# Splitting the first eight steps into float32r parts, with a new hand-written order for the first layers

## Chip, core and metric

One core of one Trainium2 chip runs the whole program. The metric is the device time of one execution in microseconds (us). The engines are named as the profile names them: PE is TensorE, DVE is VectorE, ACT is ScalarE, POOL is GpSimd, and SP issues the DMAs.

## What is computed

Three layers follow each other. The first is attention through 32 memory slots, for 4 batches `b` of 576 positions and 8 heads:

```python
a = softmax(phi, axis=2)                       # over the 576 positions
k_m = einsum('bhsm,bhsd->bhmd', a, k)          # 32 keys of 64
v_m = einsum('bhsm,bhsd->bhmd', a, v)
attn = softmax(q @ k_m.T / 8)                  # over the 32 slots
x = attn @ v_m                                 # 2304 tokens of 512, heads side by side
```

The second is a dense pair of products, and the third four weighted experts:

```python
h = x @ w_in                                   # 512 -> 2048
x = (maximum(h, 0) + alpha * minimum(h, 0)) @ w_out
for e in range(4):
    out += p[:, e:e+1] * (maximum(x @ w1[e], 0) @ w2[e])
```

`w_in` and `w_out` arrive as 64-bit floating-point numbers, which the kernel decodes on the chip into float32 before it uses them.

## The kernel before

The kernel has two parts. `run_experts` is the third layer; the diff doesn't touch it. The first two layers run before it as a list of tasks in the string `ORDER`: each name is a task, and the tasks are emitted in that order with the scheduler switched off. Each engine has its own queue and works it off in order, so the string sets, for every engine, what stands behind what.

The second layer is cut into 128 steps. A step is a block of 128 of the 2048 inner columns for half a batch (288 tokens). Step `j` counts blocks fastest (4 of them, `f`), then halves, then batches, then the four groups `c` of 512 inner columns, so steps 0 to 7 are `c=0, b=0`. The attention product with `v_m` is folded into `w_in`: `f{b}{c}{e}` (line 523) multiplies `v_m` of a batch with 256 decoded columns of `w_in` on PE, `fh` rounds the result to a float32r part (ACT, line 534), and `fl` makes the remainder (DVE, line 232). A step has these tasks:

- `u{j}`, PE: the product with the attention weights, line 559 if plain and line 562 if split
- `n{j}`, ACT: negative and positive part (lines 575 and 576), and `v{j}`, DVE: their sum with `alpha` (line 581)
- `h{j}`, ACT, rounds the result to a float32r part (line 585), and `l{j}`, DVE or POOL, makes the remainder (line 232); plain steps have neither
- `d{j}`, PE: the product with `w_out`, line 597 if plain and line 600 if split; `e{j}` copies or adds four blocks after every fourth step (lines 611 and 613)

A split product is three float32r products of rounded parts and remainders. A plain one is one float32 product, which the trace records as two matmuls. `PLAIN = 1` makes the steps with `b=0, c=0` plain, and `down` then reads the decoded `w_out` from a tile of its own.

The attention of batch `b` is a chain of small tasks for its two groups of heads `g`: `a{b}{g}_max, exp, sum, nat, natc, mem, memc, memt, memtc, sc0, sc1, ev0, ev1`, followed by the softmax over the slots, `s{b}{g}{o}_max, sub, exp, sum, mul, back, hi, lo`. For batch 0 that softmax is done in two halves of 288 columns, for the others in one piece of 576. A tile of `w_in` or `w_out` is decoded by `in{i}_0..4` and `out{i}_0..4` (lines 459, 463, 469, 470, 477 and 496), and `out{i}_5` and `out{i}_6` split it into parts (lines 500 and 232). `ON_VECTOR` names those tasks which run on DVE; of the tasks that have a choice, the others run on POOL. `w0` to `w4` are warming products on an identity matrix (line 246). `x{b}h{i}` (ACT, line 668) and `x{b}l{i}` (DVE) prepare the experts' input, `wh01` and `wl01` their first weights (ACT line 701, DVE line 232), and `sp3` stores the last batch to device memory, ahead of the experts' first weighting loads (`p<-pd`) on the SP queue.

The raw tiles go through a ring of three buffers, so that a load of one starts when the decoding of the third one before it has read its raw bytes.

Of the kernel before, what the change touches and what calls it, by code (L numbers as in the profile page):

```python
# [23 lines left out]
PLAIN = 1  # L24
# [10 lines left out]
w0 p0 pal ppr kv0 pr0 pr1 pr2 q0 w1 p1 kv1 q1 a00_max a01_max a00_exp a01_exp a00_nat a00_sum a00_natc a01_nat a01_sum  # L35
  pgates a01_nath a01_natc w2 a01_nathc a01_mem in0_1 in0_0 a00_mem in0_2 a01_memc in1_1 in0_3 out0_1 in1_0 in1_2
  a01_memt a00_memc q01 p2 a01_memtc a00_memt out0_0 in1_3 a01_sc0 a00_memtc out0_2 q2 a00_sc0 a01_ev0 in0_4 w3 a00_ev0
  s010_max in1_4 s000_max s010_sub f000 a10_max s000_sub s010_exp a11_max w4 fh000 out0_3 s000_exp a10_exp s010_sum
  out0_4 a11_exp s000_sum a10_nat s010_mul a10_sum a10_natc a11_nat s000_mul s010_back a11_nath a11_natc a11_sum
  a11_nathc s000_back in2_1 u0 out0_5 in2_0 u1 n0 in2_2 a00_sc1 n1 in2_3 a01_sc1 v0 in2_4 in3_1 d0  # L40
v1 in3_0 in3_2 in3_3 in3_4 a01_ev1 out0_6 out1_1 a00_ev1 f001 s01288_max out1_0 out2_1 a10_mem out1_2 fh001 out3_1
  out1_3 s000_hi out1_4 u2 a10_memc kv2 out2_0 d1
n2 out2_2 out1_5 out2_3 s010_hi a11_mem s00288_max in4_1 out2_4 out3_0 out2_5 v2 s00288_sub d2
s01288_sub s00288_exp out3_2 s01288_exp a11_memc out1_6 s00288_sum u3 s01288_sum a10_memt out2_6 n3 a20_max a11_memt
  a10_memtc out3_3 a11_memtc a10_sc1 a20_exp s00288_mul p3 s01288_mul a10_sc0 out3_4 in5_1 v3 out3_5 s010_lo s01288_back
  d3
s00288_back s01288_hi out3_6 s00288_hi a10_ev0 s000_lo in6_1 u4 a10_ev1 e3 s01288_lo a11_sc1 s00288_lo s100_max s100_sub
  n4 a11_sc0 a11_ev1 s100_exp v4 u5 a11_ev0 d4
s110_max n5 s110_sub s100_sum s110_exp u6 f100 v5 n6 s110_sum d5
fh100 s100_mul s110_mul u7 s100_back f101 q3 v6 s100_hi s110_back n7 d6  # L50
pst s100_lo s110_hi fl100 fh101 s110_lo a20_nat a21_max u8 v7 a21_exp u9 fl101 d7
n8 a20_sum a21_sum a20_natc v8 n9 in4_0 a21_nat h8 v9 a21_nath e7 l8 u10 in4_2 a21_natc d8
in4_3 a21_nathc in5_0 h9 in5_2 a20_mem n10 l9 v10 in5_3 h10 a21_mem l10 a20_memc in6_0 a31_max in4_4 a31_exp in6_2 d9
kv3 a21_memc in5_4 a30_max in7_1 u11 a31_sum a30_exp in6_3 a20_memt n11 a30_sum in6_4 a21_memt a20_memtc d10
a21_memtc v11 out4_1 in7_0 a20_sc0 h11 in7_2 a20_sc1 a20_ev0 l11 u12 a20_ev1 s200_max a21_sc1 n12 s200_sub a21_sc0
  a21_ev1 s200_exp v12 d11
out5_1 a21_ev0 h12 s210_max l12 u13 s200_sum e11 s210_sub u14 d12
n13 s200_mul s210_exp v13 f200 s210_sum h13 n14 l13 u15 s200_back fh200 s210_mul d13
fl200 s200_hi n15 v14 f201 s200_lo s210_back h14 s210_hi a30_nat l14 a30_natc s210_lo d14
fh201 v15 fl201 h15 u16 l15 in7_3 d15  # L60
# [7 lines left out]
s310_sum n22 l21 fh300 s300_mul d21
fh301 s310_mul in10_1 s300_back u23 v22 s300_hi s310_back h22 s300_lo s310_hi l22 n23 s310_lo d22
fl300 v23 u24 fl301 h23 n24 u25 l23 in8_0 d23  # L70
n25 v24 in8_2 h24 u26 e23 l24 v25 u27 in8_3 d24
h25 in9_0 n26 l25 in9_2 n27 d25
v26 v27 h26 u28 h27 l26 l27 d26
n28 in9_3 v28 in10_0 h28 d27
l28 in10_2 u29 e27 in10_3 u30 in8_4 d28
n29 in9_4 n30 v29 f010 h29 v30 l29 h30 u31 fh010 l30 in10_4 d29
fl010 n31 in11_1 v31 out8_1 d30
in11_0 h31 in11_2 out9_1 u32 l31 in11_3 d31
# [1030 lines left out]
```

## Time and profile before

| | |
|---|---|
| Time, median of 3 runs | 1208.26 us (1206.77 to 1208.98) |
| Profiled execution, its own time | 1206.66 us |
| Its span (first to last instruction) | 1204.7 us |
| PE busy | 1170.1 us (97%) |
| DVE busy | 782.4 us (65%) |
| ACT busy | 468.0 us (39%) |
| POOL busy | 420.2 us (35%) |

The span is 2.0 us shorter than the execution's own time. The first two layers end 418.6 us after the span's start with the last product of step 127, and the experts fill the rest. The stages have different limits, so the shares above say little about any one of them; the rows below are cut by stage.

### The profile page before, as it was taken

What the parts mean: (1) busy time and instruction counts of PE and PEld (TensorE: products, weight loads), DVE (VectorE), ACT (ScalarE), POOL (GpSimd) and SP (SyncE); (2) the same over time, 40 slices, a digit from 0 to 9 for tenths busy, and PEclk for the clock granted to TensorE, in tenths of its full rate; (3) what the DMA queues carried; (4) which work ended last, traced back from release to release, by engine and by line L of the source; (5) the groups of instructions that cost most, each with busy time, mean ns of one, the idle gap of its engine ahead of it and who ended that gap; (6) DMA issues with size and microseconds to landing.
All of it is one profiled execution on the core that took longest, in us unless ns stands there. A gap on an engine that the chain in (4) does not pass through costs nothing.

```text
span 1204.7 us, 21401 instructions
## 1 busy us (share of the span) xinstructions
PE 1170.1 (97%) x8794; PEld 1123.2 (93%) x8794; DVE 782.4 (65%) x1433; ACT 468.0 (39%) x1017; POOL 420.2 (35%) x361
## 2 busy tenths in 40 slices
PE   7799999999999989999999999989999999999998
PEld 6478899998999989999999999989999999999998
DVE  6999997685457744555566566676456656656553
ACT  4557665545455533323232223233422223232320
POOL 2212111232000054444534435465443552553430
PEclk9899999999999999999999999989999999999999
DMA  9642122010000132111112111132112111111001
GB/s 376 250 160 83 54 87 71 19 53 18 1 1 1 56 97 92 55 54 53 46 48 69 37 54 36 64 124 75 53 47 62 54 46 45 58 41 63 36 29 70
DMA packets 22994, 82.46 MB, mean 68 GB/s; under 512 B 3312, under 2 KB 4336, under 8 KB 20976
## 3 DMA queue, kind: packets, MB, share of 16 engines
q1 hardware_dynamic: 22896, 81.09, 19.8%
q8 instruction: 69, 1.13, 0.4%
q14 instruction: 29, 0.24, 0.1%
HBM read 73.97 MB, written 7.11 MB: 67 GB/s over the span
## 4 chain that ended last, share of the span: by engine, by line
PE 87%; DVE 9%; DMA 2%; ACT 1%; issue 1%; SPq 0%; ACTq 0%; DVEq 0%
PE o L823 34%; PE y L600 14%; PE uy L732 12%; PE uw L732 8%; PE ux L732 8%; PE h L562 7%; PE pw L523 2%; DMA rawin<-in_w_in 2%; PE y L597 1%; DVE g L232 1%; DVE xt L660 1%; DVE pos L581 1%; DMA p<-pd 1%; DVE min L469 0%; DVE mout L469 0%
## 5 line engine op out<-in xcount | busy, mean ns | idle before, releaser
L823 PE MATMUL o<-g,w 128*128 128x288 f32 x3072 | 450.9, 296 | 1.1 <-DVE g L232 1.1
L823 PEld LDWEIGHTS o<-g,w 128*128 128x128 f32 x3072 | 423.2, 189 | 1.8 <-DVE g L232 1.6
L232 POOL TENSOR_TENSOR w<-raww,w 128x512 fp32r<-128x512 f32 (+1 forms) x96 | 150.3, 1580 | 260.4 <-ACT w L507 155.3
L835 DVE TENSOR_TENSOR acc<-o,acc 128x288 f32<-128x288 f32 x224 | 102.1, 456 | 189.0 <-PE o L823 189.0
L600 PE MATMUL y<-g,wout 128*128 128x288 f32 x1440 | 210.1, 298 | 2.6 <-DVE g L232 1.0
L600 PEld LDWEIGHTS y<-g,wout 128*128 128x128 f32 x1440 | 195.9, 188 | 12.6 <-ACT pos L576 4.2
L732 PE MATMUL uy<-x,w 128*128 128x288 f32 x1152 | 186.0, 297 | 8.0 <-DVE v L766 8.0
L732 PEld LDWEIGHTS uy<-x,w 128*128 128x128 f32 x1152 | 164.7, 189 | 9.4 <-DVE v L766 9.3
L770 ACT COPY v<-ux 128x288 f32<-128x288 f32 x64 | 25.6, 400 | 291.8 <-PE ux L732 288.5
L801 ACT CAST g<-h 128x576 fp32r<-128x576 f32 x128 | 83.3, 676 | 139.5 <-DVE h L795 139.5
L232 POOL TENSOR_TENSOR g<-h,g 128x576 fp32r<-128x576 f32 x64 | 92.8, 1451 | 127.8 <-ACT g L801 123.0
L732 PE MATMUL ux<-x,w 128*128 128x288 f32 x768 | 123.4, 296 | 2.5 <-ACT v L770 2.5
L732 PE MATMUL uw<-x,w 128*128 128x288 f32 x768 | 123.1, 296 | 0.1
L795 DVE SCALAR_TENSOR_TENSOR h<-h,p 128x576 f32<-128x576 f32 x128 | 109.4, 855 | 6.4 <-DMA p<-pd 3.3
L562 PE MATMUL h<-a,wp 128*128 128x288 f32 x720 | 111.6, 297 | 0.3
L732 PEld LDWEIGHTS ux<-x,w 128*128 128x128 f32 x768 | 109.3, 189 | 2.7 <-ACT v L770 2.7
L732 PEld LDWEIGHTS uw<-x,w 128*128 128x128 f32 x768 | 109.3, 189 | 0.3 <-DVE y L611 0.3
L562 PEld LDWEIGHTS h<-a,wp 128*128 128x128 f32 x720 | 100.0, 188 | 5.3 <-issue 3.0
L766 DVE TENSOR_TENSOR v<-uy,v 128x288 f32<-128x288 f32 x128 | 58.5, 457 | 69.9 <-PE uy L732 69.4
L581 DVE SCALAR_TENSOR_TENSOR pos<-neg,nal,pos 128x288 f32<-128x288 f32 x120 | 64.7, 542 | 58.3 <-ACT pos L576 57.8
L575 ACT ACTIVATE neg<-h 128x288 f32<-128x288 f32 x128 | 52.8, 413 | 83.1 <-PE h L562 76.3
L232 POOL TENSOR_TENSOR g<-pos,g 128x288 fp32r<-128x288 f32 x24 | 19.7, 823 | 182.7 <-ACT g L585 134.2
(116 smaller groups left out, 1184.3 us busy)
## 6 DMA issues: line engine op xcount, KB each, us to landing
raww<-in_w SPq DMA_DIRECT2D x64, 512.0 KB, 3.7
kv<-in_kv SPq DMA_DIRECT2D x8, 1152.0 KB, 8.4
rawin<-in_w_in SPq DMA_DIRECT2D x16, 512.0 KB, 3.7
rawout<-in_w_out SPq DMA_DIRECT2D x16, 512.0 KB, 3.7
p<-pd SPq DMA_DIRECT2D x16, 288.0 KB, 4.0
q<-in_q SPq DMA_DIRECT2D x3, 1152.0 KB, 15.9
out<-acc SPq DMA_DIRECT2D x12, 288.0 KB, 2.1
pe<-in_phi SPq DMA_DIRECT2D x4, 576.0 KB, 9.0
```

What stands on the lines that cost most here:

```text
L232: eng.tensor_tensor(out=out, in0=in0, in1=in1.bitcast(F32), op=ALU.subtract)
L562: mm(p, wp_t[b, c, f // 2][:, x, o2 + g * 256:o2 + g * 256 + 128], a_t[b][:, y, g, o:o + HB], start=(n == 0), stop=(n == 5))
L575: nc.scalar.activation(out=neg, in_=p, func=AF.Relu, scale=-1.0)
L581: nc.vector.scalar_tensor_tensor(out=pos, in0=neg, scalar=nal[:, ft:ft + 1], in1=pos, op0=ALU.mult, op1=ALU.add)
L600: mm(First.acc[d], w[:, x, d * 128:(d + 1) * 128], self.gt[:, y, 0:HB], start=(self.start and n == 0), stop=(self.stop and n == 2))
L732: mm(p, w[:, x, a, k], operand(self.b, i)[:, y, k], start=(start and n == 0), stop=(n == 5), skip_group_check=not start)
L766: nc.vector.tensor_tensor(out=out, in0=x, in1=y, op=ALU.add)
L770: nc.scalar.copy(out=self.v1_t, in_=self.x)
L795: nc.vector.scalar_tensor_tensor(out=h, in0=h, scalar=0.0, in1=p_t[self.g // 2, self.b], op0=ALU.max, op1=ALU.mult)
L801: nc.scalar.copy(out=g_t[self.g, self.b, self.hp][:, i, 0], in_=h)
L823: mm(self.p, w[:, x, i, d % 2 * 128:(d % 2 + 1) * 128], g, start=(m == 0), stop=(m == 11))
L835: nc.vector.tensor_tensor(out=a, in0=self.p, in1=a, op=ALU.add)
```

## The change

There are four edits. `PLAIN` goes from 1 to 0, so steps 0 to 7 become split steps: each gets `h` and `l`, its two plain products of `u` become six float32r products, and its four plain products of `d` become twelve. Their folds get `fl000` and `fl001`. The split parts of the attention weights of batch 0 and of the first four `w_out` tiles were made before too, for other steps, and are now needed by step 0 already.

`ORDER` is written anew. The attention of batches 1 and 2 comes earlier against the steps, the decoding of `w_in` tiles 7 to 11 and `w_out` tiles 4 to 7 comes later, and `kv2` (keys and values of batch 2) is loaded ahead of `w_out` tile 2.

`ON_VECTOR` changes. `s00288`, `s01288`, `s100` and `s110` do their `sub` and `mul` on POOL now. `s000_lo`, `s00288_lo`, `s010_lo` and `s200_lo` go from POOL to DVE. `out1_6` and `out2_6` go to DVE and `out2_4` to POOL; `in0_4` and `in1_4` change places. Of the new remainders `l0`, `l2`, `l3` and `l7` are on POOL, and `l1`, `l4`, `l5` and `l6` on DVE.

The warming products change from 11, 12, 5, 5, 8 to 11, 12, 6, 5, 4.

```diff
-PLAIN = 1
+PLAIN = 0
...
-v1 in3_0 in3_2 in3_3 in3_4 a01_ev1 out0_6 out1_1 a00_ev1 f001 s01288_max out1_0 out2_1 a10_mem out1_2 fh001 out3_1
...
+  a20_memt a21_memc a20_memtc a21_memt a20_sc0 a21_memtc a10_ev1 out2_5 out3_2 d0
...
-    for i, n in enumerate((11, 12, 5, 5, 8)):
+    for i, n in enumerate((11, 12, 6, 5, 4)):
```

On PE, at the first step. In the kernel before, two plain `u` products (`h`) and a score product (`pc`) stand ahead of step 0's plain `d` products (`y00000` to `y00003`, the first of the four is shown), then a fold and the memory products of batch 1 (`pm10`):

```order
L559 MATMUL h0000_400<-pe0_133,wp000_352 128x288 x2
L559 MATMUL h0001_406<-pe0_133,wp000_352 128x288 x2
L357 MATMUL pc001_415<-q0_147,kt00_301 64x288 x2
L357 MATMUL pc011_425<-q0_147,kt01_287 64x288 x2
L597 MATMUL y00000_433<-g0000_410,wholeout0_363 128x288
...
L523 MATMUL pw001_455<-win0_313,vt00_302 64x256 x2
L523 MATMUL pw001_455<-win0_313,vt01_288 64x256 x2
L325 MATMUL pm10_466<-kv10_164,pe1_162 32x128 x18
```

In the kernel after, on the same engine just ahead of step 0's first `d` products:

```order
L562 MATMUL h0003_606<-a0_422,wp001_555 128x288 x6
L305 MATMUL pnh2_619<-ident_102,pe2_280 64x128
L306 MATMUL pnh2_619<-ident_102,pe2_280 128x128
L325 MATMUL pm20_631<-kv20_417,pe2_280 32x128 x18
L325 MATMUL pm20_631<-kv21_418,pe2_280 32x128 x2
...
L342 MATMUL pt21_723<-ident_102,kvb21_713 128x128 x2
L357 MATMUL pc200_727<-q2_319,kt20_719 64x288 x2
L600 MATMUL y00000_739<-g0000_569,wout0_426 128x288 x3
```

The products of batch 2's memory (`pm20`, `pm21`) and its first scores (`pc200`) now stand ahead of step 0, and steps 0 to 3 have their `u` products done before it.

On DVE, at steps 16 and 17 (`pos0200`, `pos0201`). Before, between their sums, `w_out` tiles 4 and 5 are decoded (`mout`, `sout`):

```order
L581 SCALAR_TENSOR_TENSOR pos0200_1209<-neg0200_1208,nal_104,pos0200_1209 128x288
L469 SCALAR_TENSOR_TENSOR mout4_994<-mout4_994,sout4_995 128x512
L470 TENSOR_SCALAR sout4_995<-mout4_994 128x512
L232 TENSOR_TENSOR g0200_1221<-pos0200_1209,g0200_1221 128x288
L477 SCALAR_TENSOR_TENSOR sout4_995<-rawout4_879,sout4_995 128x512
L459 TENSOR_SCALAR sout5_1047<-rawout5_957 128x512
L496 TENSOR_TENSOR win1_913<-min7_942,sin7_943 128x4x128
L496 TENSOR_TENSOR mout4_994<-mout4_994,sout4_995 128x512
L581 SCALAR_TENSOR_TENSOR pos0201_1263<-neg0201_1262,nal_104,pos0201_1263 128x288
```

After, at the same two steps, softmax work of batch 3 (`rs310`, `pe3`):

```order
L581 SCALAR_TENSOR_TENSOR pos0200_1384<-neg0200_1383,nal_104,pos0200_1384 128x288
L394 TENSOR_REDUCE rs310_1400<-pe3_653 128x18
L395 TENSOR_SCALAR rs310_1400<-rs310_1400 128x18
L396 RECIPROCAL rs310_1400<-rs310_1400 128x18
L402 TENSOR_TENSOR pe3_653<-pe3_653,rs310_1400 128x576
L232 TENSOR_TENSOR g0200_1418<-pos0200_1384,g0200_1418 128x288
L581 SCALAR_TENSOR_TENSOR pos0201_1412<-neg0201_1411,nal_104,pos0201_1412 128x288
```

The decoding of those `w_out` tiles has moved to a place behind step 21.

On ACT, at the end of the second layer. Before, the last two castings of the experts' input (`x15`) stand between the last steps' parts (`g3312`, `g3313`) and the experts' first weights (`w101`):

```order
L585 CAST g3312_5037<-pos3312_4989 128x288
L668 CAST x15_5040<-xt1_4795 128x576
L585 CAST g3313_5043<-pos3313_5034 128x288
L668 CAST x15_5040<-y1_1066 128x576
L701 CAST w101_5090<-raww11_3148 128x768
```

After:

```order
L585 CAST g3312_5141<-pos3312_5108 128x288
L575 ACTIVATE neg3313_5144<-h3313_5111 128x288
L576 ACTIVATE pos3313_5145<-h3313_5111 128x288
L585 CAST g3313_5175<-pos3313_5145 128x288
L701 CAST w101_5208<-raww11_3617 128x768
```

Those two castings are done before step 118's product now, and nothing stands between the last step's part and the weights.

## Rows read from the trace of the kernel before

**Rows 1.** The page: span, and PE's busy time, share and instructions.

```profile
span 1204.7 us, 21401 instructions
PE 1170.1 (97%) x8794; PEld 1123.2 (93%) x8794; DVE 782.4 (65%) x1433; ACT 468.0 (39%) x1017; POOL 420.2 (35%) x361
```

**Rows 2.** Stages: from:to, length, busy us (instructions) by engine, clock, DMA, GB/s.

```profile
0.00:28.20 28.20, 22.11 (x202) 18.34 (x202) 18.47 (x46) 12.78 (x31) 6.63 (x17) 0.94 0.94 373
28.20:78.50 50.30, 43.08 (x272) 30.00 (x276) 46.09 (x90) 29.53 (x73) 8.06 (x7) 0.93 0.51 191
78.50:136.20 57.70, 52.28 (x490) 43.15 (x491) 56.34 (x106) 37.88 (x100) 14.80 (x13) 1.00 0.32 114
136.20:200.00 63.80, 63.72 (x475) 60.04 (x474) 56.05 (x113) 41.22 (x105) 9.47 (x8) 1.00 0.24 76
200.00:418.60 218.60, 217.69 (x1607) 203.21 (x1606) 146.17 (x295) 113.19 (x283) 33.23 (x33) 1.00 0.07 23
418.60:434.90 16.30, 12.67 (x79) 11.62 (x78) 7.60 (x15) 3.88 (x8) 5.08 (x5) 0.90 0.54 173
```

**Rows 3.** Chain that ended last, start and length, first 150 us.

```profile
36.27 0.76 DVE pe L362 x2
...
137.80 1.59 PE y L600 x12
139.39 1.58 PE h L562 x12
```

**Rows 4.** Timeline of PE: start, length, what, idle before it.

```profile
54.16 3.70 PE L597 MATMUL y<-g,wholeout 128*128 128x288 f32 x8 [2.00 <-DVE g L581]
...
65.17 2.21 PE L597 MATMUL y<-g,wholeout 128*128 128x288 f32 x8
67.22 1.13 PE L559 MATMUL h<-pe,wp 128*128 128x288 f32 x4
68.28 1.08 PE L523 MATMUL pw<-win,vt 128*64 128x256 f32 x8
...
78.43 2.80 PE L325 MATMUL pm<-kv,pe 128*32 128x128 f32 x80
```

**Rows 5.** Timeline of DVE: first row of one tile's decoding and of the next.

```profile
37.29 0.41 DVE L459 TENSOR_SCALAR sout<-rawout 128x512 uint32<-128x512 uint32 x1
...
40.33 0.42 DVE L459 TENSOR_SCALAR sout<-rawout 128x512 uint32<-128x512 uint32 x1
```

**Rows 6.** DVE and POOL groups, first 140 us: count, busy us, mean ns.

```profile
L232 DVE TENSOR_TENSOR g<-pos,g 128x288 fp32r<-128x288 f32 x13 | 7.3, 564 | 0.0
L385 DVE TENSOR_TENSOR pe<-pe,mx 128x576 f32<-128x576 f32 x5 | 3.7, 748 | 0.1
L385 POOL TENSOR_TENSOR pe<-pe,mx 128x576 f32<-128x576 f32 x1 | 1.2, 1169 | 0.0
L232 POOL TENSOR_TENSOR g<-pos,g 128x288 fp32r<-128x288 f32 x4 | 3.6, 900 | 11.0 <-ACT g L585 11.0
L232 POOL TENSOR_TENSOR wout<-wholeout,wout 128x512 fp32r<-128x512 f32 x3 | 4.3, 1427 | 15.1 <-ACT wout L500 15.1
```

**Rows 7.** Timeline of POOL and of DVE beside it, at two places.

```profile
20.66 1.59 POOL L385 TENSOR_TENSOR pe<-pe,mx 128x288 f32<-128x288 f32 x2 [4.27 <-DVE mx L379]
46.20 1.97 POOL L232 TENSOR_TENSOR a<-pe,a 128x288 fp32r<-128x288 f32 x2
...
21.36 1.40 DVE L276 TENSOR_REDUCE nm<-pe 128x1 f32<-128x576 f32 x2
46.47 2.02 DVE L385 TENSOR_TENSOR pe<-pe,mx 128x288 f32<-128x288 f32 x2
```

**Rows 8.** Timeline of ACT: a wait for the second `w_out` tile's load.

```profile
36.43 0.67 ACT L463 ACTIVATE mout<-rawout 128x512 f32<-128x512 f32 x1 [3.42 <-DMA rawout<-in_w_out]
```

**Rows 9.** Chain that ended last, from the second layer into the experts.

```profile
414.62 0.57 ACT x L668
415.52 0.58 ACT x L668
```

More of the change, by code (lines that the diff above doesn't have):

```diff
@@ L41 @@
-v1 in3_0 in3_2 in3_3 in3_4 a01_ev1 out0_6 out1_1 a00_ev1 f001 s01288_max out1_0 out2_1 a10_mem out1_2 fh001 out3_1
[L42 to L60, printed above, removed]
@@ L68 @@
[L68 to L78, printed above, removed]
@@ new lines @@
+l17 a30_ev1 out4_1 s300_max n19 v18 d17
+s300_sub h18 l18 s300_exp u20 v19 s300_sum h19 d18
+n20 l19 s310_back u21 v20 s300_mul f300 h20 n21 l20 s300_back d19
+fh300 v21 s300_hi fl300 h21 u22 s300_lo e19 u23 l21 out4_0 f301 in6_3 n22 d20
+in7_0 s310_hi v22 h22 s310_lo n23 d21
+l22 fh301 v23 in6_4 d22
+fl301 h23 l23 out5_1 u24 in7_2 u25 n24 out4_2 d23
+n25 v24 v25 h24 u26 in7_3 e23 u27 l24 out4_3 f010 h25 out4_4 n26 d24
+l25 n27 v26 in7_4 h26 u28 v27 out4_5 d25
+l26 h27 out5_0 n28 l27 out5_2 out6_1 d26
@@ new lines @@
+out14_1 v73 fl220 h73 h74 l73 u76 l74 n75 d73
+out14_0 n76 v75 out14_2 h75 u77 l75 d74
+v76 n77 out13_3 h76 d75
+v77 l76 h77 out13_4 u78 l77 e75 out13_5 u79 n78 out13_6 f221 n79 v78 u80 v79 h78 h79 u81 l78 l79 n80 d76
+out14_3 fh221 v80 n81 fl221 out14_4 d77
+h80 v81 out14_5 l80 d78
+h81 out14_6 l81 out15_3 d79
+ws00 u82 e79 u83 n82 f320 n83 u84 fh320 d80
+fl320 v82 v83 h82 d81
+out15_4 h83 l83 out15_5 l82 u85 n84 out15_6 wopen d82
+n85 v84 h84 v85 wh00 d83
+l84 u86 e83 h85 wl00 u87 n86 f321 d84
@@ new lines @@
+l85 fh321 v86 n87 fl321 ws01 d85
+h86 u88 u89 f030 f031 fh030 l86 v87 n88 d86
+fl030 h87 v88 fh031 l87 u90 h88 fl031 n89 l88 d87
+v89 n90 u91 h89 e87 l89 u92 n92 v90 d88
+h90 v92 l90 h92 d89
+n91 l92 v91 u93 h91 d90
+l91 n93 v93 d91
+h93 l93 u94 e91 u95 n94 f130 n95 v94 h94 d92
+v95 fh130 l94 h95 fl130 d93
+l95 u96 u97 n96 d94
+n97 v96 h96 v97 d95
+l96 h97 l97 u98 e95 u99 n98 f131 n99 v98 h98 d96
+v99 fh131 l98 h99 fl131 d97
+l99 d98
+u100 u101 n100 d99
+n101 v100 h100 v101 u102 l100 e99 h101 u103 l101 n102 f230 n103 v102 d100
@@ new lines @@
+h102 v103 fh230 l102 h103 fl230 d101
+l103 u104 d102
+n104 v104 d103
+h104 l104 u105 e103 u106 n105 f231 n106 v105 x0t0 h105 u107 fh231 l105 d104
+v106 n107 fl231 h106 v107 u108 x0h0 l106 x0t1 h107 u109 n108 l107 d105
+x0t2 n109 v108 x0h1 v109 d106
+h108 x0t3 h109 l108 x0h4 d107
+l109 x0h5 x0l1 x0l5 u110 e107 u111 n110 f330 n111 v110 d108
+v111 h110 h111 l110 fh330 l111 d109
+x0h2 fl330 x0h3 x0l2 d110
+x0l3 x0l4 u112 x0l0 x0h6 d111
+n112 x0l6 v112 u113 e111 h112 u114 l112 n113 f331 n114 v113 x1t0 h113 d112
@@ new lines @@
+fh331 v114 l113 h114 fl331 d113
+x1h0 l114 x1l0 u115 x1t1 d114
+n115 x1t2 v115 u116 x1t3 h115 u117 l115 n116 d115
+n117 v116 h116 v117 u118 l116 h117 e115 u119 l117 n118 n119 u120 v118 d116
+v119 h118 h119 l118 l119 n120 d117
+x1h5 v120 h120 x1l5 d118
+x1h6 l120 x1l6 u121 d119
+n121 v121 u122 e119 h121 u123 l121 n122 n123 u124 v122 sp2 h122 d120
+v123 l122 h123 n124 l123 d121
+v124 h124 d122
+l124 d123
+x1h3 x1h4 x1l3 u125 e123 x1h1 u126 n125 n126 u127 v125 x1l4 h125 d124
+x1h2 v126 l125 h126 x1l1 n127 d125
@@ L175 @@
+l126 v127 x1l2 d126
+h127 l127 to wh01 d127
 wl01 e127 sp3
```

202 lines of the change are left out of this document (84 added, 118 removed).

## Prediction

> **What bounds the kernel now.** I read the page first, then the stages, then the chain of waits. The span of 1204.7 us lies in an execution of 1206.66, with PE busy for 97% [rows 1]. The stages show where that share hides something. Up to 28.2 us the loads bind (DMA share 0.94). From there to the end of step 8 (78.5 us) DVE is busy for 46.1 of 50.3 us, and from step 8 to the end of step 22 (136.2 us) for 56.3 of 57.7. From then on PE is busy for 63.7 of 63.8 and 217.7 of 218.6 us, with DVE at 88% and then 67%. Between the second layer and the experts (418.6 to 434.9) PE is busy for 12.7 of 16.3 us [rows 2]. The chain of waits agrees: DVE pieces follow each other around 36 us, and PE pieces alone around 138 us [rows 3].
>
> So step 22 is the hinge. Behind it PE has the same tasks in both orders, all split and at the same price; ahead of it PE has the same tasks too, but for the eight steps and the warming. The end therefore moves by as much as the end of step 22 moves, plus what changes later beside PE. I work out that end on two paths, DVE's and PE's, and the later one decides.
>
> **The eight steps on PE.** A plain `d` takes 65.17 to 67.22, 2.05 us, and a plain `u` 67.22 to 68.28, 1.06 [rows 4]. A split `d` is a chain piece of 1.59 us, and two split `u` are one of 1.58 [rows 3], 0.79 each. Three short products are thus cheaper than one plain one: 3.11 - 2.38 = 0.73 us a step, 5.8 us for eight. But they lie where DVE binds, so this isn't yet a gain. The 38 warming products in place of 41 fill waits, and I cost them at nothing: what hides them is the load-bound stage.
>
> **DVE up to step 22.** Decoding one tile takes 37.29 to 40.33, 3.04 us [rows 5]. By the order, most of the decoding of five tiles (`in7`, `out4` to `out7`) leaves this stretch: 5 x 3.04, less two first pieces (0.41 each) and one sum (0.7) that don't move, plus two splits (0.7): 15.1 us. New are `fl000`, `fl001`, `fl300` (0.7 each, like the 576-wide row), `l1`, `l4`, `l5`, `l6` (0.56 each) and one step's sum (0.5): 4.9 us. Engines change: `sub` and `mul` of two 576-wide softmaxes (4 x 0.75) and of two halves (4 x 0.38) go to POOL; three halved `lo` (0.38), one full one (0.75) and a net one of the `w_out` pieces (0.7) come: -2.0 us [rows 3, 6]. That is -12.2; since some of the 3.04 is latency between dependent pieces, which mixing hides anyway, I take -11.5 (ends -10.8 and -12.2). POOL's own sum up to there grows by under 1 us. DVE's path: 136.2 - 11.5 = 124.7 us.
>
> **DVE and POOL up to step 8.** Here the new order puts more ahead. On DVE: three `fl` 2.1, four `l` 2.3, four transpositions of batch 2's scores 1.5, six 576-wide passes for batches 2 and 3 4.5, small ones 1, less two pieces of `in4` 1.5, less 2.7 for changed engines: +7.2 by row means. Neighbours overlap by some 0.07 us, so I take +6.5. On POOL: four `l` at 0.90, five 576-wide passes at 1.17, four halves at 0.80 and a sum of some 1.3 come, two splits of 1.43 and three `lo` of 0.90 go: +8.4 us [rows 6, 7].
>
> POOL's time costs DVE something. DVE's two maxima beside POOL's passes took their usual 1.40 us (21.36); two subtractions beside POOL's (46.47) took 2.02 us in place of about 0.75, so they stood until POOL was done [rows 7]. The price of 8.4 us is thus between 0, if only reductions and transpositions stand beside it, and 8.4. The softmax alternates both kinds, so I take half, 4.2. [...]
>
> Against this stands DVE's idle time of 4.2 us between 28.2 and 78.5 [rows 2], part of which an order with more ready work fills; I take 2 (0 to 4.2). Step 8 then ends at 78.5 + 6.5 + 4.2 - 2 = 87.2 us. Ends: 78.5 + 6.5 - 4.2 = 80.8, and 78.5 + 6.5 + 8.4 = 93.4.
>
> **PE from step 8 to step 22.** In the new order there stand 14 `d` (1.59, 22.3 us), 12 `u` (9.5), two folds (2.0), two memory products (2.7, the row at 78.43) and 18 small plain products of batch 3's transpositions and scores (a fold's four take 1.0, so at most 0.25 each; I take 3.5 us): 40.0 us [rows 3, 4]. The batch 2 products that were here before stand ahead of step 8 now. DVE is left with 56.3 - 11.5 - 6.5 = 38.3 us in the same stretch, nearly as much as PE, so some latency shows on PE: 0 to 5 us, I take 2.5. PE's path: 87.2 + 40.0 + 2.5 = 129.7 us. It is the later one, so step 22 ends at 129.7 in place of 136.2, -6.5 (ends: 80.8 + 40.0 = 120.8, held up by DVE's 124.0 at the least, so -12.2; 93.4 + 45 = 138.4, +2.2).
>
> **Behind step 22.** The decoding that was put off lies beside PE from here on. DVE has 7.8 us free up to 200 us and 72 us up to 418.6 [rows 2], so it is hidden if it is spread; where it is bunched PE waits: 0 to 3 us, I take 0.5. At the end of the second layer the chain ran through two castings on ACT (0.57 and 0.58 us) [rows 9] that stand elsewhere now. The experts' first weights, the last sums and the gates' load behind them come that much earlier: -1.1 us (0 to -2.5; PE's idle in that stage is 3.6 us, and the clock's share of 0.90 [rows 2] may rise with a shorter idle). `run_experts` is unchanged, and so are its transfers.
>
> **Sum.** -6.5 + 0.5 - 1.1 = -7.1 us: 1206.66 becomes 1199.6. The median of the runs before is 1.6 us above the profiled execution, so I predict 1208.26 - 7.1 = 1201.2. A measurement of this kernel can tell about 0.2%, 2.4 us, from no change.
>
> **Rivals.**
>
> *POOL costs DVE little and the idle time is filled.* Step 8 ends near 81, PE's path gives 122 to 123, and DVE's path of 124.0 to 125.4 binds: -11.5 with the rest -0.6, 1196. For it: PE has batch 2's memory done before step 0 and steps 0 to 3 prepared, so fewer chains are open at once; against it: POOL gets twice what it did up to step 8.
>
> *POOL stops DVE in full.* Step 8 ends at 78.5 + 6.5 + 8.4 - 2 = 91.4, step 22 at 133.9, -2.3 - 0.6: 1205.4. For it: the subtractions at 46.47; against it: the maxima at 21.36 [rows 7]. [...]
>
> *PE stands in front of batch 2.* Step 0 now queues behind `pm20` and `pm21`, which need `kv2`. The second `w_out` tile landed at 36.4 us [rows 8], the same loads are ahead of `kv2`, and its 2.36 MB at 373 GB/s [rows 2] end at 42.7; then come two more tiles, whose casts stand ahead of `pm20`'s copies on ACT, the copies, transpositions and scores: step 0 at about 52 us. From there PE has 26 us up to step 8 (nine `d`, eight `u`, three folds, 2.5 us of small products), 78 us, under DVE's 87. It decides from step 0 at 61 us on. If PE's idling before it drops the clock, as it did at 54.16, where a plain `d` took 3.70 us after 2.0 of idle [rows 4], four steps at half the speed cost 9.5 us more. Step 0 at 65 and that: 100.5 at step 8, 143 at step 22, +6.8 - 0.6, 1214.5, slower.
>
> *The steps get cheaper but nothing reaches the end*: DVE's list, not PE's, holds step 22 with the decoding still ahead of it. The order rules that out: the pieces stand behind step 21.
>
> **How the numbers follow.** The forecast, 1198 to 1204: 0.45. Little cost on POOL, 1192 to 1198: 0.25. Full stops, 1204 to 1208: 0.20, half of it within 0.2%. PE in front of batch 2, from 1208 on: 0.10, nearly all of it slower. Faster by over 0.2% (below 1205.8): 0.45 + 0.25 + 0.10 = 0.80; within 0.2%: 0.11; slower: 0.09. The range 1194 to 1208 leaves out the last rival and part of the second.
>
> **What would show it.** Right: split steps 0 to 7 with `d` pieces of 1.6 us; the end of step 8 later than 78.5, near 87; the end of step 22 near 130, with PE close to full from step 8 on; the second layer's end near 412; DVE above 85% up to 130. Wrong: step 8 not later than before (the second term is too dear), step 22 after 136, or idle PE behind step 22 with DVE named as what ended it. Step 0 after 61 us would make the third rival right.

## Result and profile after

The changed kernel takes 1190.3 us (median of 4 runs, 1189.17 to 1194.06) beside 1207.7 for the kernel before (4 runs): a ratio of 0.9861, with a 95% interval from 0.9836 to 0.9885. It gained 17.4 us. I had forecast 7.1, a time of 1201.2, and a range down to 1194. The direction was right and the size was not. The two profiled executions are 16.7 us apart by their spans, and the parts below add up to that.

The page of the profiled execution (1189.82 us), which answers to [rows 1]:

```profile
span 1188.0 us, 21509 instructions
PE 1161.2 (98%) x8836; PEld 1122.3 (94%) x8836; DVE 777.4 (65%) x1436; ACT 470.1 (40%) x1025; POOL 425.9 (36%) x368
```

The stages, cut at the ends of the same steps as in [rows 2] (the columns are the same):

```profile
0.00:28.20 28.20, 22.63 (x244) 18.61 (x244) 18.02 (x46) 13.84 (x34) 6.54 (x17) 1.00 0.95 376
28.20:83.50 55.30, 47.97 (x404) 36.42 (x397) 49.91 (x105) 36.37 (x95) 15.85 (x16) 0.91 0.55 215
83.50:124.70 41.20, 41.20 (x365) 37.03 (x364) 38.86 (x75) 28.79 (x76) 8.03 (x7) 1.00 0.13 40
124.70:200.00 75.30, 75.30 (x561) 70.44 (x561) 65.25 (x128) 48.68 (x123) 14.40 (x11) 1.00 0.24 78
200.00:404.70 204.70, 204.56 (x1519) 192.50 (x1518) 146.64 (x300) 109.15 (x275) 32.47 (x33) 1.00 0.10 33
404.70:421.00 16.30, 13.69 (x100) 12.99 (x99) 9.06 (x19) 4.75 (x10) 6.18 (x4) 1.00 0.52 174
```

Read the PE column against the length: from step 8 (83.5 us) to the end of the second layer PE has 0.1 us of free time. Before, the stage behind step 8 was DVE's, with PE busy for 52.28 of 57.70 us. The granted clock between the layers is 1.00 where it was 0.90. The ends of the steps in both traces, beside the forecast:

| | before | after | moved | forecast |
|---|---|---|---|---|
| step 0, start | 32.3 | 54.1 | | about 52 |
| step 8, end | 78.5 | 83.5 | +5.0 | +8.7 |
| step 22, end | 136.2 | 124.7 | -11.5 | -6.5 |
| step 127, end | 418.6 | 404.7 | -13.9 | -6.0 |
| from there to the end of the span | 786.1 | 783.3 | -2.8 | -1.1 |

One trace fixes such an end to about 1 us: in the seven traces of this study that have the changed kernel's program up to step 8, it ends between 83.4 and 84.8, and in the four that have the old order up to there between 78.4 and 79.5.

The chain that ended last (start, length, what) answers to [rows 3] and [rows 9]:

```profile
33.64 9.80 DMA rawout<-in_w_out
...
54.20 5.50 PE y L600 x36
...
64.54 0.66 PE pc L357 x4
...
75.45 2.31 DVE a L232 x2
77.81 1.32 PE h L562 x8
...
84.30 4.76 PE y L600 x36
...
406.81 6.27 DMA p<-pd
```

Up to 53 us it is mostly loads and DVE, then PE up to 65.2, then DVE up to 77.8 us, and PE alone from there until 377. The last row is the gates' load in front of the experts. In the kernel before, PE stood in the chain from 54.2 to 73.5 us, mostly DVE held it from there to 134.5, and behind that ACT and DVE pieces still came in at four places between 164 and 275 us:

```profile
54.16 3.70 PE y L597 x8
...
71.94 1.60 PE h L562 x12
...
134.50 1.73 PE y L600 x11
...
265.15 1.15 DVE wout L232
```


POOL beside DVE in the new order (start, length, what) answers to [rows 7]:

```profile
51.36 1.27 POOL L496 TENSOR_TENSOR mout<-mout,sout 128x512 f32<-128x512 f32 x1 [0.62 <-DVE sout L477]
51.61 0.43 DVE L408 STREAM_TRANSPOSE pe<-pe 128x288 f32<-128x288 f32 x1
...
67.36 1.21 POOL L402 TENSOR_TENSOR pe<-pe,rs 128x576 f32<-128x576 f32 x1 [3.83 <-ACT g L585]
67.47 1.42 DVE L232 TENSOR_TENSOR g<-pos,g 128x288 fp32r<-128x288 f32 x1
69.98 0.40 DVE L232 TENSOR_TENSOR g<-pos,g 128x288 fp32r<-128x288 f32 x1
```

The transposition at 51.61 took 0.43 us beside POOL's addition, its usual time (0.43 too at 52.70, with POOL free). The subtraction at 67.47 took 1.42 us beside POOL's pass; the same one at 69.98, begun while POOL was free, took 0.40.

### The profile page after: what moved, and what is told of

Its sections match the earlier page's. It is cut to its first block, busy times and chain, and to the rows that moved or that the text cites. A ratio compares the mean times of both kernels' runs of the same rounds, so it can differ in the third digit from the quotient of the medians.

```text
span 1188.0 us, 21509 instructions
## 1 busy us (share of the span) xinstructions
PE 1161.2 (98%) x8836; PEld 1122.3 (94%) x8836; DVE 777.4 (65%) x1436; ACT 470.1 (40%) x1025; POOL 425.9 (36%) x368
## 4 chain that ended last, share of the span: by engine, by line
PE 91%; DVE 4%; DMA 4%; ACT 1%; issue 0%; SPq 0%; DVEq 0%; ACTq 0%
PE o L823 34%; PE y L600 17%; PE uy L732 13%; PE uw L732 8%; PE ux L732 8%; PE h L562 8%; PE pw L523 2%; DMA rawin<-in_w_in 2%; DMA rawout<-in_w_out 1%; DVE xt L660 1%; DMA p<-pd 1%; DVE g L232 1%; PE pc L357 0%; PE pm L325 0%; DVE x L232 0%
## 5 line engine op out<-in xcount | busy, mean ns | idle before, releaser
L600 PE MATMUL y<-g,wout 128*128 128x288 f32 x1536 | 219.7, 298 | 0.2 <-DVE g L232 0.2
L600 PEld LDWEIGHTS y<-g,wout 128*128 128x128 f32 x1536 | 208.0, 189 | 11.3 <-ACT pos L576 5.0
L801 ACT CAST g<-h 128x576 fp32r<-128x576 f32 x128 | 83.4, 676 | 139.1 <-DVE h L795 139.0
L562 PE MATMUL h<-a,wp 128*128 128x288 f32 x768 | 117.5, 297 | 0.7 <-DVE a L232 0.5
L562 PEld LDWEIGHTS h<-a,wp 128*128 128x128 f32 x768 | 106.2, 188 | 5.4 <-ACT pos L576 3.1
L581 DVE SCALAR_TENSOR_TENSOR pos<-neg,nal,pos 128x288 f32<-128x288 f32 x128 | 71.7, 562 | 51.0 <-ACT pos L576 50.5
L232 POOL TENSOR_TENSOR g<-pos,g 128x288 fp32r<-128x288 f32 x29 | 23.9, 828 | 197.0 <-ACT g L585 155.3
## 6 DMA issues: line engine op xcount, KB each, us to landing
q<-in_q SPq DMA_DIRECT2D x3, 1152.0 KB, 16.3
```

What stands on the lines that cost most here:

```text
L232: eng.tensor_tensor(out=out, in0=in0, in1=in1.bitcast(F32), op=ALU.subtract)
L562: mm(p, wp_t[b, c, f // 2][:, x, o2 + g * 256:o2 + g * 256 + 128], a_t[b][:, y, g, o:o + HB], start=(n == 0), stop=(n == 5))
L581: nc.vector.scalar_tensor_tensor(out=pos, in0=neg, scalar=nal[:, ft:ft + 1], in1=pos, op0=ALU.mult, op1=ALU.add)
L600: mm(First.acc[d], w[:, x, d * 128:(d + 1) * 128], self.gt[:, y, 0:HB], start=(self.start and n == 0), stop=(self.stop and n == 2))
L801: nc.scalar.copy(out=g_t[self.g, self.b, self.hp][:, i, 0], in_=h)
```

## Experiments

Each kernel differs from the kernel before or from the changed one by the edit shown.

### What the split and the order are worth apart

`split_only` has the old order with the first eight steps split; what these steps need is moved ahead of them, and `l1`, `l4`, `l5` and `l6` are on DVE as in the changed kernel.

```diff
-PLAIN = 1
+PLAIN = 0
...
 fh000
+fl000
...
+s000_hi s010_hi s000_lo s010_lo
 u0
 out0_5
+out0_6
...
 v0
+h0 l0
...
```

> The kernel before with steps 0 to 7 split into parts and nothing else of the new order: h and l of these steps behind their v, fl000 and fl001 behind fh000 and fh001, and the splits that these steps need (s000, s010, s00288, s01288 and the four w_out tiles) moved ahead of them. PE loses 8 x 0.73 = 5.8 us; DVE gets two fl of 0.7 and four l of 0.4, +3.0 us, POOL four l of 0.8. Theory A (DVE's list sets the end of step 8 in the order of before): step 8 from 78.5 to about 81.5, the total the same to +3 us, 1208 to 1211. Theory B (PE's list sets it): -5.8 us, 1202.

`order_only` has the new order, with its list `ON_VECTOR` and its warming products, but plain steps. "The order" below means all three; no run parts them, but for the eight passes of `pool_back`.

```diff
-PLAIN = 0
+PLAIN = 1
...
-fl000
...
-fl001
...
-h0
...
-l0
```

> The new order with plain float32 products in steps 0 to 7: h0 to h7, l0 to l7, fl000 and fl001 left out. PE gets 8 x 0.73 = +5.8 us from step 0 on, DVE loses 2 x 0.7 + 4 x 0.4 = 3.0 us. Theory A (DVE's list sets the end of step 8 in the new order too, the step of the prediction): step 8 from 83.4 to 80.4 or no later than 83.4, total 1187 to 1190.3. Theory B (in the new order PE binds from step 0 at 54 us on, where it idles for less than 1 us up to 83.5): step 8 at 89, total +5.8, 1196.

`split_only` took 1216.6 us against 1207.84 (ratio 1.007, 1.0053 to 1.0087), and `order_only` 1193.66 (0.9883, 0.9858 to 0.9908). So the split costs 8.8 us in the old order, and the order alone gains 14.2. In the new order the split gains 3.4 by the medians, but the two intervals overlap; by the traces it is about 1 to 2 us (step 127 ends at 406.9 in `order_only`, and between 404.5 and 406.1 in five traces with the split). In the old order theory B is out and theory A didn't go far enough: step 0 starts at 37.9 instead of 32.3 and step 8 ends at 87.0, later than theory A's 81.5. The waits of PE between 28 and 70 us say why (who waited for whom, us in total, times, longest):

```profile
PE h L563 <- ACT a L416: 3.9, 1, 3.9
PE y L601 <- ACT wout L501: 2.5, 2, 1.3
PE pw L524 <- DVE pe L363: 2.1, 1, 2.1
PE y L601 <- POOL wout L233: 2.0, 2, 1.0
```

A split step needs the parts of the attention and of `w_out` finished ahead of it, and in the old order PE comes to them too early. In the new order step 8 ends at 85.6 with plain steps, 0.8 to 2.2 us later than with split ones:

```profile
53.70:85.60 31.90, 31.90 (x160) 22.91 (x159) 24.19 (x48) 16.98 (x42) 7.24 (x6) 0.97 0.32 118
```

PE is busy for all of its 31.9 us from step 0 to step 8, so there the steps' price counts, though not in full: eight `d` and four `u` in that stretch differ by 4.8 us, at my prices of a step. My sentence that the cheaper steps are no gain where DVE binds fails for the new order.

### The decoding that was put off

`decode_early` is the changed kernel with that decoding spread between steps 15 and 21.

```diff
-h17 a30_ev0 n18 d16
+h17 a30_ev0 out4_3 n18 d16
-l17 a30_ev1 out4_1 s300_max n19 v18 d17
+out4_4 l17 in7_4 a30_ev1 s300_max out4_5 n19 v18 out5_0 d17
...
```

> The changed kernel with the decoding of in7 and out4 to out7 (and the end of in6) moved back ahead of step 22, spread between steps 15 and 22. DVE gets about 12 us in the 41.2 us from step 8 to step 22, of which 38.9 are busy. Theory A (the decoding that was put off is what DVE's list held PE with): step 22 from 124.6 to 134, total +8 to +10, 1198 to 1200, unless PE regains part of it behind step 22 from the shorter list there. Theory B (DVE's order is loose enough, PE alone sets step 22): 1190.3.

`late_decode` is the kernel before with the tiles from `in7` and `out4` on, and the experts' first weight parts, at the steps where the new order has them.

```diff
-kv3 a21_memc in5_4 a30_max in7_1 u11
+kv3 a21_memc in5_4 a30_max u11
...
+l16 in7_1 u17
...
```

> The kernel before with only the decoding put off: in7 and out4 to out7, and the tiles behind them, stand at the steps where the new order has them (and the first experts' weight parts ws00, wh00, wl00, ws01 with them, eight steps later); steps 0 to 7 stay plain float32. DVE loses 15 us up to step 22, so it ends at 121 by its list; PE has 52.3 us of work between step 8 and step 22 and step 8 stays at 78.5. Theory A (PE then binds): step 22 at 130.8, -5.4, and up to -2.3 behind it, total 1200 to 1203. Theory B (DVE's list alone sets step 22, as in the prediction's first path): step 22 at 124.7 or less, total 1194 to 1197. Theory C (the decoding was hidden): 1208.

`decode_early` took 1203.7 us (0.9972, 0.996 to 0.9984), 13.4 above the changed kernel; step 22 ends at 137.9 and step 127 at 418.0, so all of it reaches the end. I had expected 8 to 10. The stage from step 8 to step 22, and the same two stages of `late_decode` (step 8 to 22, step 22 to 127):

```profile
84.10:137.90 53.80, 46.16 (x365) 39.13 (x364) 50.46 (x98) 32.06 (x82) 10.36 (x9) 0.94 0.27 79
```

```profile
78.60:132.10 53.50, 51.05 (x491) 42.96 (x491) 42.30 (x82) 32.64 (x90) 10.05 (x10) 1.00 0.19 74
132.10:423.40 291.30, 284.87 (x2078) 263.69 (x2077) 215.13 (x431) 160.16 (x398) 46.79 (x44) 1.00 0.14 43
```

This confirms the hinge: 13.2 us more at step 22 are 13.3 at step 127. DVE's busy time in the stage grew by 11.6 us (38.86 to 50.46). Behind step 22 `decode_early` takes 280.1 us and the changed kernel 280.0, so there the decoding that was put off costs nothing. But `late_decode` took 1211.73 us (1.0033, 1.002 to 1.0046), slower than the kernel before. Step 22 came 4.1 us earlier, limited by PE as theory A has it, and then 8.9 us were lost up to step 127 (291.3 where the kernel before takes 282.4): PE waits there for the parts of `g` from DVE (3.2 us), POOL (1.9) and ACT (0.7), 5.8 us in all. All three theories were too low in time. I read it as pieces put off into a list that wasn't laid out for them, where they stand ahead of what the steps need; no run isolates that, and 2.2 of the 8.9 us come behind step 80, about as much as the moved weight parts cost there by themselves (`ws_late`, below).

### The price of POOL's passes

`after_again` is the changed kernel once more. `pool_back` returns eight passes to DVE (in the list `ON_VECTOR`), and `pool_more` gives POOL seven more.

> The changed kernel itself once more, as the yardstick for the kernels that differ from it by one edit. Expected: 1190 us (1189 to 1192), step 0 from 54.1 us on, end of step 8 near 83.5, end of step 22 near 124.7, end of step 127 near 404.7 on the trace.

```diff
+s00288_mul s00288_sub s01288_mul s01288_sub s100_mul s100_sub s110_mul s110_sub
```

> The changed kernel with sub and mul of the softmaxes s00288, s01288, s100 and s110 back on DVE, as before the change; the order stays. DVE gets 4 x 0.75 + 4 x 0.38 = +4.5 us up to step 8, POOL loses 4 x 1.17 + 4 x 0.80 = 7.9 us. Theory A (a pass on POOL costs DVE nothing, and DVE binds up to step 8): step 8 from 83.5 to 88.0, total +4.5, 1194.8. Theory B (half of POOL's time is lost to DVE, the term of the prediction): +4.5 - 4.0 = +0.5, 1190.8. Theory C (DVE stands for all of POOL's time): -3.4, 1186.9. Theory D (PE, not DVE, binds from step 0 on, since in the changed kernel PE idles for under 1 us between 54.1 and 83.5): nothing or up to +2, as far as the later results reach PE.

```diff
-l4
-l5
-l6
-out2_6
-out3_6
-s100_lo
-s110_lo
```

> The changed kernel with seven more differences on POOL: l4, l5, l6, out2_6, out3_6, s100_lo and s110_lo. DVE loses 3 x 0.40 + 2 x 0.69 + 2 x 0.70 = 4.0 us up to step 8, POOL gets 3 x 0.81 + 2 x 1.29 + 2 x 1.48 = 8.0 us. Theory A (POOL free of charge, DVE binds): step 8 at 79.5, total -4.0, 1186.3. Theory B (half price): 0. Theory C (full price): +4.0, 1194.3. Theory D (PE binds from step 0 on): step 8 stays at 83.5 or moves later by the longer latency of these parts on POOL (0.4 to 0.8 us each), 1190.3 to 1192.

They took 1190.28 us (0.9852, 0.9838 to 0.9867), 1190.67 (0.9852, 0.9837 to 0.9867) and 1192.25 (0.9866, 0.9851 to 0.9881). Step 8 ended at 83.4, 84.0 and 83.3. The stretches up to step 0 and from there to step 8, of `after_again`, `pool_back` and `pool_more` (look at DVE, the third busy figure, and POOL, the fifth):

```profile
28.20:54.10 25.90, 18.26 (x243) 12.62 (x236) 24.52 (x56) 19.52 (x52) 6.78 (x8) 0.96 0.86 341
54.10:83.50 29.40, 28.60 (x196) 24.26 (x196) 26.51 (x52) 18.16 (x46) 9.05 (x8) 0.96 0.29 107
```

```profile
28.20:54.10 25.90, 18.92 (x200) 12.76 (x198) 24.66 (x59) 17.60 (x48) 4.46 (x4) 0.78 0.85 340
54.10:83.50 29.40, 28.72 (x198) 23.75 (x197) 27.20 (x56) 18.79 (x48) 3.87 (x4) 0.96 0.29 108
```

```profile
28.20:54.10 25.90, 16.45 (x212) 10.84 (x209) 24.79 (x58) 18.85 (x50) 6.85 (x9) 1.00 0.84 334
54.10:83.50 29.40, 29.28 (x199) 25.16 (x199) 24.53 (x47) 18.89 (x49) 16.69 (x15) 0.94 0.31 118
```

With 7.5 us of POOL gone and 4.5 us of passes added, DVE's busy time grew by only 0.8; with 7.7 us of POOL added and 4.0 us of passes gone it fell by only 1.7. To part work from stalls I counted DVE's instructions in program order up to the last one listed ahead of `d8`, and took for each the median of its form where POOL is idle as its own work, and what it took beyond that as stalled:

| up to `d8`, us | own work | stalled | idle | list ends | POOL busy |
|---|---|---|---|---|---|
| before | 54.2 | 8.6 | 9.3 | 76.6 | 12.6 |
| after | 59.6 | 7.5 | 11.0 | 82.7 | 21.0 |
| `after_again` | 59.7 | 7.9 | 10.5 | 82.6 | 21.0 |
| `pool_back` | 63.5 | 5.7 | 9.5 | 83.3 | 13.6 |
| `pool_more` | 56.4 | 8.5 | 12.6 | 82.1 | 28.4 |

The sum of own work and stalls, the idle time and the end come straight from the trace. How the sum is parted depends on which instructions count as one form: other groupings put the change of the stalls from before to after anywhere between -1.9 and +0.8 us. What they all show is that the stalls did not grow by some 4 us.

Within the new order 3.8 us of own work taken off POOL moved the list's end by 0.7, and 3.3 us given to it by -0.5. Net, a microsecond on POOL costs about 0.4 us, 0.1 to 0.3 of it as stalls and the rest as idle time. In the seven traces that are the same up to step 8 the list ends between 82.6 and 84.0, so the 0.4 is uncertain by about 0.2. Theory B, half, is nearest in both runs. A and C are ruled out by the list: from 82.6 A would have moved its end to 86.4 and 79.3, C to 79.0 and 86.7, and it is 83.3 and 82.1. D isn't told apart from B here, since step 8 stayed within the spread. The 2.0 us by which `pool_more` is above `after_again` lie elsewhere: its step 127 ends at 404.6, like the other's 404.5, and the gap behind it ran at a granted clock of 0.85 in place of 1.00 (below).

### Does step 0, or a load, hold the first steps?

`d0_early` moves step 0 ahead of batch 2's memory products, and `kv2_behind` the load of `kv2` behind two tiles of `w_out`.

```diff
+a10_ev1 a10_ev0 a11_ev0 a11_ev1
 out2_1
...
+d0
 a20_mem
```

> The changed kernel with step 0 ahead of batch 2's memory products instead of behind its scores, and the four evacuations of batch 1's scores (which hold the banks that step 0 needs) ahead of the third w_out tile on DVE. PE idles 2.8 us between 45 and 54 and its granted clock is 0.69 there. Theory A (PE's list binds from step 0 on, and step 0 only waits in line): the 1.6 us of step 0 fill that idle time, step 3 ends at 62.9 in place of 64.4, step 8 at 82, total -1.5, 1188.8. Theory B (DVE's list still sets step 8): no change, 1190.3. Theory C (with step 0's four banks taken, batch 2's products wait for the two that are left): step 8 later than 83.4, up to 87, 1194.

```diff
-kv2
 fl000
...
 in3_3
+kv2
```

> The changed kernel with batch 2's kv loaded behind the third and fourth w_out tile instead of ahead of them. In the changed kernel the chain of waits runs through the fourth piece of that queue (33.64, 9.80 us, the w_out tile behind kv2), but DVE idles only 0.5 us for it at 43.46. Theory A (that load sets step 0): step 0 from 54 to 51, total -2 to -3, 1188. Theory B (DVE's list sets step 0; the load only comes last in the record): within 1 us, 1190.3. Theory C (kv2 then lands too late for batch 2's memory products at 45.9): step 0 later by 2 to 6 us, 1193 to 1196.

Neither moved step 8 forward. In `d0_early`, which also has the four tasks `a10_ev0` to `a11_ev1` earlier, step 0 starts at 44.9, but step 3 ends at 65.1 (64.4 in `after_again`) and step 8 at 84.1, within the spread. PE waits for batch 2's copies in both kernels (`kvb`, 1.4 and 1.3 us here and 1.4 and 1.2 in `after_again`); two waits of 0.5 us on the copies `vt` are new, and the granted clock between 54 and 65 us is 0.81 instead of 0.88. Theory A is out. The new waits are of theory C's kind, but at this size B and C aren't told apart. It took 1194.01 us (0.9886, 0.9867 to 0.9904), in runs that spread from 1190.4 to 1196.3. `kv2_behind` took 1190.31 us (0.9861, 0.9848 to 0.9874), theory B: the 9.80 us in the chain came last in the record, but DVE was busy for 8.85 us of it.

### Behind step 22

`ws_late` is the kernel before with the experts' first weight parts eight steps later. `tail_after` is the kernel before up to step 22, with the remaining tasks in the new order and on its engines.

```diff
-ws00 fh121 out15_5
+fh121 out15_5
...
-u80 d79
+ws00 u80 d79
```

> The kernel before with the first experts' weight parts (ws00, wopen, wh00, wl00, ws01) eight steps later, at steps 80 to 85 as in the new order. Theory A (they bunch with the last decoding on POOL, ACT and DVE at steps 68 to 76, where the kernel before loses 2.3 us that the new one doesn't): from step 64 to step 80 44 us in place of 46.0, total -2.0 to -2.3, 1205.5. Theory B (the loss there comes from the order of the steps' own pieces): 46.0 us, 1207.8.

```diff
-fl300 v23 u24 fl301 h23 n24 u25 l23 in8_0 d23
+fl300 v23 fl301 h23 l23 u24 u25 n24 d23
...
```

> The kernel before, its order unchanged up to step 22; behind it the tasks that are left stand in the new order (the tiles in7 and out4 to out7 are decoded by then, so DVE has some 15 us less to do there than in the changed kernel). Theory A (the new order behind step 22 is itself the better one): step 22 at 136.2, step 127 at 416.2 in place of 418.6, gap with the shorter wait, total -2.4 - 1.0, 1204.4. Theory B (the gain behind step 22 comes from what stands ahead of it): step 127 at 418.6, total -1.0, 1206.7. If the lighter DVE helps beyond that, step 127 comes before 416.

`ws_late` took 1208.89 us (1.0017, 1.0008 to 1.0026): no gain from step 64 to 80 (45.7 us, before 46.0), and 2.3 us more behind it. My explanation by those parts falls. In the changed kernel and in `tail_after` these sixteen steps take 43.9 us. `tail_after` took 1203.14 us (0.9966, 0.9954 to 0.9979). From step 22 to step 127, in the kernel before, the changed one and `tail_after`:

```profile
136.20:418.60 282.40, 281.42 (x2079) 263.25 (x2078) 202.22 (x407) 154.41 (x388) 42.70 (x41) 1.00 0.11 35
```

```profile
124.70:404.70 280.00, 279.86 (x2077) 262.94 (x2077) 211.89 (x427) 157.83 (x396) 46.87 (x44) 1.00 0.14 45
```

```profile
137.30:417.30 280.00, 279.86 (x2079) 262.95 (x2078) 199.55 (x406) 153.31 (x388) 42.56 (x42) 1.00 0.11 35
```

The new order behind step 22 makes those 2.4 us itself, 2.1 of them between steps 64 and 80. The old order left PE idle for 1.0 us there, and PE was busy for 1.6 us longer with as many products. What stretched them stays open; the rows name waits of 0.6 us only. The chain of the kernel before runs through DVE in these steps (a `w_out` remainder at 265.15), and that of the changed kernel through PE alone.

### The gap in front of the experts

`x_tail` moves the last two operands back to the end of the second layer (in the changed kernel their castings stand ahead of the products of steps 118 and 119). `gates_first` issues the gates' first loads ahead of the last spill; `gates_first_2` is the same kernel beside `after_third`, the changed kernel, on one chip.

```diff
-x1h5 v120 h120 x1l5 d118
+v120 h120 d118
...
-l126 v127 x1l2 d126
+l126 v127 x1h5 x1l2 d126
...
```

> The changed kernel with the last two operands of batch 1 (x1h5, x1h6, x1l5, x1l6) back at the end of the second layer, where they stood before the change. If their place made the shorter gap between the second layer and the experts, the time from the end of step 127 to the end of the span grows from 783.3 to 786.1 us, the measured difference: 1193.1. If my term was right it grows by 1.1: 1191.4. If the gap shortened for another reason (TensorE's granted clock there was 0.90 before and 1.00 after), the time stays at 1190.3 and the clock tells.

```diff
-    def run_experts():
-        load_gates(0, 0)
-        load_gates(0, 1)
+    def first_gates():
+        load_gates(0, 0)
+        load_gates(0, 1)
+
+    def run_experts():
...
+    task("lg", first_gates)
...
-h127 l127 to wh01 d127
+h127 l127 to lg wh01 d127
```

> The changed kernel with the experts' first two gate loads issued ahead of the last spill (behind the task to, where the pool opens) in place of behind it. In the changed kernel the chain of waits between the second layer and the experts runs through that load (406.81, 6.27 us), and PE waits there for 2.6 us in two waits of 1.5 and 1.1. Theory A (the load behind the spill is what sets the gap): the rest behind step 127 falls from 783.4 to 781 to 782, total 1188 to 1189, and TensorE's granted clock there stays 1.00. Theory B (the vector pieces of the last step, 402.92 to 405, set it): 783.4, 1190.3.

> The changed kernel with the experts' first gate loads ahead of the last spill, once more and beside the changed kernel on the same chip. Theory A (the load behind the spill holds the first expert product): PE's wait of 1.5 us ends and the time is 1.0 to 1.9 us below the changed kernel's. Theory B (the gap's other waits take its place): no difference, within 0.5 us.

> The changed kernel once more, as the yardstick on the same chip: 1190.3 us (1189.2 to 1192.4), the wait before the first expert product 1.5 to 1.6 us.

PE's longest wait behind step 127, at a `ux` product of the first expert, in the changed kernel and in `x_tail`:

```profile
PE ux L732 <- ACT v L770: 1.5, 1, 1.5
```

```profile
PE ux L733 <- ACT v L771: 2.7, 1, 2.7
```

In the kernel before it is 2.5. So the operands' place is worth 1.0 to 1.2 us in that wait, my term. `x_tail` took 1192.7 us (0.9877, 0.9858 to 0.9896), 2.4 above `after_again`; in its trace 1.8 us of that lie behind step 127 and about 1 ahead of step 8, where the two programs are the same. What is left of the 2.8 us may go with the granted clock (0.90 before, 1.00 after). The 16.3 us behind step 127 in `pool_more`, `x_tail` and `ws_late` (the clock is the third figure from the end):

```profile
404.60:420.90 16.30, 13.42 (x83) 12.61 (x82) 7.40 (x17) 3.88 (x8) 5.56 (x4) 0.85 0.54 174
```

```profile
405.50:421.80 16.30, 12.46 (x88) 11.53 (x87) 8.53 (x17) 3.88 (x8) 4.90 (x5) 1.00 0.55 174
```

```profile
420.40:436.70 16.30, 12.49 (x89) 11.57 (x88) 8.63 (x17) 3.88 (x8) 5.00 (x5) 1.00 0.53 173
```

`pool_more` has the same tasks there as the changed kernel and a wait of 1.8 us, a granted clock of 0.85 in place of 1.00, and takes 786.4 us instead of 783.3 from step 127 to the end. The other way round, `ws_late` has the tasks of the kernel before at a clock of 1.00, and takes 785.1 instead of 786.1 at 0.90. So with the operands in their old place and a clock of 1.00 `x_tail` and `ws_late` take 1.8 us more than the changed kernel, and the clock goes with about 1 us more. No run changed the clock by itself.

`gates_first` took 1188.43 us (0.9848, 0.9833 to 0.9863) and `gates_first_2` 1188.53 (1187.91 to 1189.52) beside 1190.87 of `after_third` (1190.02 to 1191.83): 2.3 us less, a little above theory A's 1.9. The wait for `ux`, 2.2 us in the trace of `after_third` where I had expected 1.5 to 1.6, is gone, and one row is left:

```profile
PE uy L733 <- DVE v L767: 1.1, 2, 0.6
```

This is the fastest kernel of the study.

## Why the prediction was wrong in size, point by point

**The hinge** was right. The end of step 22 moved by 11.5 us, and in `decode_early` 13.2 us at step 22 became 13.4 at the end. But it sets only two thirds of the gain here (11.5 of 16.7 us).

**The eight steps.** The prices held (0.73 us a step). "No gain yet" didn't: in the new order PE binds behind step 8 and is nearly level with DVE ahead of it, so the split is worth 1 to 3 us. The reading that these steps lie where DVE binds was too coarse from the start: in the chain of the kernel before PE stands from 54.2 to 73.5 us.

**DVE's list up to step 22** was right. Own work fell by 11.0 us by the count above taken up to `d22` (103.8 to 92.8; 10 to 14 by other groupings), where I took 11.5.

**DVE and POOL up to step 8** is the term that was mis-sized most: +8.7 forecast, +5.0 measured, 3.7 us. I had +6.5 of own work, +4.2 of stalls and -2 of idle time; the count shows +5.4, -1.1 and +1.7, 6.0 at the end of the list. The step that failed is the +4.2: the new order has 8.4 us more of POOL, as I summed, and the stalls changed by -1.9 to +0.8 us, however they are counted. The -2 for idle time was wrong too, in the other direction. Half a price for one more microsecond of POOL was not far off within the new order (about 0.4), so I read the mistake as adding it to the old order's stalls as if these stayed.

Why they didn't stay is open. The rows suggest a reason, which no run isolated: a subtraction beside a POOL pass took 1.42 us (67.47) where the same one with POOL free took 0.40 (69.98), while a transposition beside a pass took its usual 0.43 us (51.61). What stands beside POOL's passes would then set the price. If DVE had stood for all of POOL's added time it would have made 8.4 us; the count has -1.1.

**PE from step 8 to step 22** took 41.2 us, busy throughout. My list was 40.0 and the 2.5 us of latency on top didn't show: 1.3 us of the miss.

**Behind step 22** I had +0.5 and measured -2.4: 2.9 us of the miss. I read 217.69 of 218.6 us busy as full and looked only for what the change could lose there. `tail_after` shows that the order itself was worth 2.4, and `decode_early` that the decoding put off cost nothing there.

**The gap.** I had -1.1 and measured -2.8. The wait shrank by 1.0 us, as forecast. By `x_tail` and `ws_late` the old place of the operands goes with 1.8 us in all, and the granted clock (0.90 before, 1.00 after), which I left as a remark, with about 1 us. These misses, 3.7, 1.3, 2.9 and 1.7 us, make up the 9.6 between the forecast of 7.1 and the 16.7 of the traces.

**The rivals.** What happened is nearest to *POOL costs DVE little and the idle time is filled* in its result at step 22 (-11.5, its very figure). That is chance: it had DVE's path bind there, and PE's did, with PE busy throughout; the idle time was not filled and POOL is not cheap. It lacked the last two terms too. *POOL stops DVE in full* is ruled out by the list's end in both POOL runs. Step 0 at 54.1 us stayed under the 61 from which *PE stands in front of batch 2* decides.

## What to carry to other kernels

A stage that looks 99% busy can still hold a few microseconds that a better order takes out (2.4 us here), so a new order's effect on it needs a term that can be negative. Work that is made cheaper and the order around it aren't additive: here the split alone cost 8.8 us, the order alone gained 14.2, and together they gained 17.4. When passes go to another engine, don't add their price to the old order's stalls: what stands beside them changes with the order (here the stalls changed by -1.9 to +0.8 us, where I had added 4.2).

## What I had not expected of the hardware

With much the same idle time of PE behind the second layer (1.5 to 2.7 us in its longest wait; the kernels with the gates first are left out), the granted clock of the following 16.3 us was 0.84 to 0.90 in five of the traces and 1.00 in the others. In the kernel before, where it was 0.90, the trace has 0.50 from 430.2 to 433.6, right behind the wait of 2.5 us that ended at 430.2, and 1.00 for the rest. With the same tasks there, the traces at the lower figure took 1 to 3 us longer from step 127 to the end. Within one kernel the measured times spread by about as much (1205.15 to 1209.38 for the kernel before). Ahead of the end of step 8 the granted clock was 0.50 in places too, as in the kernel before from 54.7 to 58.1 us, where PE had been idle for 2.0 us up to 54.2, and in the changed kernel from 48.5 to 55.3, where PE had been idle for 1.2 us up to 48.5.

Short DVE instructions stood beside POOL too: a `TENSOR_SCALAR` on 128x2 numbers took 1.12 us at 25.14 in the changed kernel, beside a POOL pass from 24.97 to 26.23, and 0.23 at 74.57, where POOL was idle.
